# An RWKV-7 and token-mixing kernel: v of the first eight tiles loaded in long runs and turned back by TensorE, the last output row in two column parts

## The chip, the core and the metric

The kernel runs on one core of one Trainium2 chip. Its time is the device time of one execution in microseconds (us). The core has five engines that run side by side and wait for each other by semaphores: PE (TensorE, matrix multiplies and transposes, results in PSUM), DVE (VectorE), ACT (ScalarE), POOL (GpSimd) and SP, which here only issues transfers. Sixteen DMA engines carry the transfers of SP's and POOL's queues. PSUM has eight banks.

## The reference, cut to what matters

A recurrent state of 40 x 40 is kept for each of 4 batches and 8 heads over 768 steps; its read-out is the input of a token-mixing layer over 320 channels.

```python
for t in range(S):                                   # S = 768, D = 40
    y[:, :, t] = einsum('bhd,bhde->bhe', r[t], state)
    Sa = einsum('bhde,bhe->bhd', state, a[t])
    state = state * w[t] - einsum('bhd,bhe->bhde', Sa, b[t]) + einsum('bhd,bhe->bhde', v[t], k[t])
x = y as [4, 768, 320]
theta = x @ w_theta
y2 = einsum('ts,bsd->btd', w_tok_r, x * cos(theta)) + einsum('ts,bsd->btd', w_tok_i, x * sin(theta))
u = x + y2
out = u + maximum(u @ w_ch, 0)
```

The six inputs r, k, v, w, a, b are fp32, [4, 8, 768, 40] each: a head's step is a run of 40 numbers (160 bytes), and the steps of one head follow each other in memory.

## The kernel before, in words

**Tiles.** The work is cut into 24 tiles of 128 steps, six to a batch, tile i = 6 * batch + position. For a tile, w, k, b, a and v are each loaded with the 128 steps on the partitions and the eight heads side by side, 160 KB in 1024 runs of 160 bytes (`load`, L497, issued at L635). r is loaded differently, for two tiles at once (a pair): eight successive steps of a head lie together in memory, so a partition takes a run of 1280 bytes (L644, two issues of 128 runs for a pair). The rows then stand in another order, eight steps on one partition; one copy makes bf16 of them (L715), eight PE transposes turn them (L723), and two strided copies on ACT put each tile's steps in order (L727), which gives r transposed. r is needed in that form only.

**One tile's work.** `prep` (L653): ACT takes the log of w (L659), PE sums it over the steps (L666 to L674), ACT exponentiates (`ex`, L678). k, b and a are multiplied by the result on POOL (L686, L690; on DVE for the first two tiles). v is copied to bf16 as it lies (L695, on ACT for tiles 0 and 1, on POOL after). PE transposes k and b, a and v (L616) and ACT copies the results out of PSUM (L619: kbT, aT, vT). v is needed in both forms: transposed for the scores against r (`lamv`), and as it lies as a multiplier in the recurrence (x0 at L779, the state update gt at L809). `attention_scores`, `recurrence` and `readout` follow: four 128 x 1024 masked products on DVE (L745), x0, nu, the state gt, and the read-out y, which becomes x (L879). `theta` (L888) and the sines (L912, ACT) give z = x * cos and x * sin (L924, POOL). The sines need another ACT table than log and exp; a switch is a table load (L912, L1039).

**Rows.** When a batch's six tiles have their z, its six output rows of 128 steps can be made (`mix_row`, L932): 12 matmuls of 320 columns with w_tok (L942), u = x + row (L952), three transposes of u (L843) and a copy (L619, uT), three matmuls with w_ch (L888), out = max + u (L961, `oo`), and the store (L964, SP). w_tok is loaded by POOL's queue in six blocks (L982) and transposed on PE (L990) during the first six tiles. The rows of one batch are worked on while the next batch's tiles go on.

**Order.** Every step is an operation of a planner (`Plan.order`, L98). It simulates the five engines with the costs given to `add`, and at each turn takes the ready operation of an engine with the lowest priority number, where waiting costs `WAIT` and a table switch `TSWITCH`. A priority is the tile's or row's base time (`TIMES`) plus the kind's offset (`OFF`) plus a number for the single operation (`ADJ`). The result is a fixed instruction order for each engine and each queue; SP's loads are ordered in the same way, and a load also waits until its buffer is free (raw_v has six, one a tile). A PSUM bank is taken when a PE operation starts and freed when its readers are done; single banks are four. Some operations of the start have dummy matmuls put before them (`WARM`).

Of the kernel before, what the change touches and what calls it, by code (L numbers as in the profile page):

```python
# [24 lines left out]
SP_DEPTH = 3600.0  # L25
WARM = {("tv", 0): (512, 512, 512, 512, 512, 512, 256), ("cs", 0): (256, 128),
# [205 lines left out]
def tail(n):  # L232
# [4 lines left out]
    ah=-35.84, ch=48.62, cs=-41.07, ea=8.9, egd=-133.96, egt=-68.6, ekb=29.91, enu=-49.74,  # L237
    enut=-31.32, er=-1.07, eth=-44.84, eut=-81.74, ev=34.77, ewt=-21.29, ex=-16.18, exp=-69.77,
    ext=-70.75, gd=-0.66, gt=24.57, kb=0.69, la=-21.49, lb=-20.79, lk=-21.05, ln=-58.38,
    loadr=-19.57, lv=-18.31, lw=-23.25, mlu=77.8, mlv=20.57, mphi=99.76, mpsi=106.6, nu=-4.03,  # L240
    nut=17.1, nx=-102.76, oo=44.39, r=13.19, row=39.85, sin=86.4, slu=-21.92, slv=29.13,
    sphi=-34.9, spsi=-25.62, st=34.46, ta=-13.27, th=35.87, tkb=6.76, tr=-5.45, tv=13.16,
    uadd=-11.95, ut=33.59, v=-54.81, wdma=85.37, wt=32.27, x0=-18.91, xt=5.58, y=-25.18,
    z=50.36)
WAIT, TSWITCH, PSWITCH = 398.44, 188399.0, -3357.0
TIMES = dict(
    tile=[
        -65.18, -52.14, -27.19, -15.19, -0.09, 16.27, 18.34, 39.82, 40.75, 43.08, 49.45, 52.18,
        68.94, 83.98, 96.98, 120.81, 109.42, 127.8, 136.07, 145.79, 151.2, 162.31, 163.45,
        185.34],  # L250
    row=[
        43.16, 28.13, 30.47, 7.23, 53.69, 54.58, 93.52, 93.6, 115.41, 121.11, 101.85, 144.65,
        150.48, 155.04, 152.8, 117.63, 86.15, 91.69, 209.97, 231.59, 245.27, 311.99, 320.81,
        183.2],
    rel=[
        -80.1, 35.36, 62.13, 56.14, -154.77, 90.95, 23.01, 50.8])
ADJ = {
    0: 0.01, 1: -0.88, 2: -0.27, 3: -0.13, 4: -9.48, 5: 1.93, 6: 0.01, 7: -6.64, 8: -6.95,
    9: 2.16, 10: -0.5, 11: 4.59, 12: 0.14, 13: 0.14, 14: -2.05, 15: 1.86, 16: 1.1, 17: 0.1,
    18: 0.09, 19: -1.57, 20: -11.2, 21: 2.84, 22: -9.69, 23: 4.35, 24: 11.96, 25: -7.67,  # L260
    26: -8.16, 27: -0.64, 28: 7.64, 29: -2.2, 30: 9.61, 31: -5.25, 32: -7.79, 33: 1.01,
    34: 0.1, 35: 13.97, 36: 2.59, 37: 8.9, 38: -2.75, 39: -7.81, 40: -5.57, 41: -1.21,
    42: -0.06, 43: 0.97, 44: 0.99, 45: 4.55, 46: -1.08, 47: 23.46, 48: 0.44, 49: 12.19,
    50: -0.53, 51: 9.26, 52: -2.79, 53: 0.97, 54: -23.89, 55: 7.88, 56: 2.16, 57: 5.54,
    58: 1.4, 59: 0.22, 60: 1.28, 61: -5.88, 62: -2, 63: -5.35, 64: 13.13, 65: -1, 66: 0.41,
    67: -1.73, 68: 4.62, 69: -0.84, 70: -7.71, 71: -0.16, 72: 4.87, 73: -0.18, 74: 3.79,
    75: 4.43, 76: 0.74, 77: 0.06, 78: 6.38, 79: -6, 80: -2.91, 81: 0.43, 82: 3.27, 83: 3.51,
    84: -0.44, 85: -2.07, 86: -2.74, 87: -2.44, 88: 2.94, 89: -22.98, 90: 3.09, 91: 9.21,
    92: -2.91, 93: 18.56, 94: 11.17, 95: -1.31, 96: -4.33, 97: -0.08, 98: 3.45, 99: 0.12,
    100: -1.86, 101: -0.16, 102: -12.32, 103: 7.19, 104: -6.11, 105: 0.71, 106: -14.73,  # L270
    107: -16.11, 108: -1.26, 109: -2.12, 110: -11.67, 111: 2.03, 112: -15.5, 113: -2.82,
    114: -4.71, 115: -1.47, 116: -2.37, 117: -4.76, 118: 13.45, 119: 10.68, 120: -10.01,
    121: 0.33, 122: 3.27, 123: -1.43, 124: 0.58, 125: -0.44, 126: -0.16, 127: -0.19,
    128: -0.03, 129: 9.47, 130: 3.96, 131: -3.42, 132: 7.74, 133: 20.39, 134: -13.3, 135: -2.8,
# [796 lines left out]
```

## Time and profile before

| | us |
|---|---|
| median of 7 executions | 213.9 (212.45 to 214.21) |
| profiled execution, device time | 213.41 |
| its span, first to last instruction | 211.6 |
| PE busy / ACT busy / POOL busy | 198.8 / 152.6 / 117.6 |
| hardware queue (SP): share of the 16 DMA engines' time | 66.8% |

How to read it: an engine is busy while one of its instructions runs; PE's matmuls overlap, so busy does not mean at its peak. PEld is PE's loading of weights beside the matmuls. The DMA share is the mean busy share of the sixteen DMA engines in a stretch. A group line gives line, engine, operation, written and read tile, shape and count, then total busy us and mean ns of one, then idle time before them with what ended it. The chain of waits follows from the last instruction back to what released each step: start, length, what.

### The profile page before, as it was taken

Reading aid. Unit: us, or ns where it says so; the run is one execution under the profiler, and the core shown is the slowest. Engines: PE = TensorE matmul, PEld = TensorE weight load, DVE = VectorE, ACT = ScalarE, POOL = GpSimd, SP = SyncE. Lnnn points to the kernel's source line nnn. Section 1 sums busy time; section 2 is a strip of 40 time slices with the busy share of each in tenths; the row PEclk is TensorE's granted clock in tenths of the full one; section 3 lists DMA queues with packets and bytes.
Section 4 is the critical chain, followed back from the end, with each engine's and each line's share of the span. In section 5 each row is a group of like instructions: output and inputs, shape, how many; then the busy total and the mean of one; then the engine's idle time right before and its main releaser. Section 6 shows DMA issues by size and latency. Waiting matters only on the chain.

```text
span 211.6 us, 8102 instructions
## 1 busy us (share of the span) xinstructions
PE 198.8 (94%) x3365; PEld 155.4 (73%) x3365; DVE 166.3 (79%) x253; ACT 152.6 (72%) x342; POOL 117.6 (56%) x173
## 2 busy tenths in 40 slices
PE   7787999979999999999999999999999999999993
PEld 3465787757777788788787877788778787877761
DVE  7587778896979799789898677877889898946343
ACT  4475777999799868977948789777898757573011
POOL 3205365779878674885971859773658440751000
PEclk9999999999999999999999999999999999999998
DMA  7999999899999999995989889989895101002122
GB/s 121 196 159 193 158 190 180 136 199 179 181 175 181 187 188 203 187 165 68 260 160 194 166 155 211 161 183 174 187 197 111 34 3 33 2 3 94 67 91 93
DMA packets 134181, 30.82 MB, mean 146 GB/s; under 512 B 125824, under 2 KB 134144, under 8 KB 134144
## 3 DMA queue, kind: packets, MB, share of 16 engines
q1 hardware_dynamic: 131712, 27.54, 66.8%
q0 software_dynamic: 2432, 2.77, 8.6%
q8 instruction: 26, 0.43, 0.9%
q14 instruction: 11, 0.09, 0.1%
HBM read 29.13 MB, written 3.93 MB: 156 GB/s over the span
## 4 chain that ended last, share of the span: by engine, by line
PE 73%; DMA 8%; POOL 6%; SPq 6%; ACT 3%; issue 2%; DVE 0%; POOLq 0%; ACTq 0%; DVEq 0%
PE ps_s L942 19%; PE ps_s L616 12%; PE ps_d L740 9%; PE ps_s L888 9%; SPq L635 5%; PE ps_s L843 4%; POOL kb L686 3%; DMA wrow_r<-in_moe_w_tok_r_dram 3%; DMA raw_v<-in_v_dram 2%; DMA raw_w<-in_w_dram 2%; PE ps_s L723 2%; PE ps_s L809 2%; PE ps_s L791 2%; PE ps_s L990 2%; PE ps_s L872 2%
## 5 line engine op out<-in xcount | busy, mean ns | idle before, releaser
L686 POOL TENSOR_TENSOR kb<-raw_kb,ex 128x320 bf16<-128x320 f32 x44 | 37.2, 862 | 17.5 <-ACT ex L678 17.3
L942 PE MATMUL ps_s<-zr,wtok_r 128*128 128x320 bf16 x144 | 41.0, 300 | 0.0
L942 PE MATMUL ps_s<-zi,wtok_i 128*128 128x320 bf16 x144 | 40.9, 299 | 0.0
L690 POOL TENSOR_TENSOR ah<-raw_a,ex 128x320 bf16<-128x320 f32 x22 | 19.0, 864 | 29.6 <-issue 15.6
L745 DVE TENSOR_TENSOR lamu<-ps_d,mask_p 128x1024 bf16<-128x1024 f32 x24 | 29.3, 1220 | 7.5 <-PE ps_d L740 7.1
L745 DVE TENSOR_TENSOR phi<-ps_d,mask_n 128x1024 bf16<-128x1024 f32 x24 | 29.2, 1219 | 4.5 <-PE ps_d L740 4.2
L745 DVE TENSOR_TENSOR lamv<-ps_d,mask_p 128x1024 bf16<-128x1024 f32 x24 | 29.2, 1218 | 4.0 <-PE ps_d L740 3.8
L745 DVE TENSOR_TENSOR psi<-ps_d,mask_p 128x1024 bf16<-128x1024 f32 x24 | 29.2, 1216 | 1.5 <-PE ps_d L740 1.5
L924 POOL TENSOR_TENSOR zi<-cs,x 128x320 bf16<-128x320 f32 x23 | 17.7, 790 | 10.1 <-ACT cs L912 9.9
L924 POOL TENSOR_TENSOR zr<-cs,x 128x320 bf16<-128x320 f32 x23 | 17.7, 791 | 6.8 <-ACT cs L912 6.8
L678 ACT ACTIVATE ex<-ps_d 128x648 f32<-128x648 f32 x24 | 17.1, 713 | 4.8 <-PE ps_d L674 3.6
L619 ACT COPY uT<-ps_s 128x192 f32<-128x192 f32 x24 | 7.5, 318 | 15.5 <-PE ps_s L843 14.2
L879 DVE TENSOR_TENSOR x<-ps_s,ex 128x320 bf16<-128x320 f32 x24 | 11.7, 486 | 8.1 <-PE ps_s L872 4.0
L942 PEld LDWEIGHTS <-wtok_r 128*128 128x128 bf16 x144 | 14.0, 98 | 4.5
L740 PE MATMUL ps_d<-aT,kbT 64*128 64x128 bf16 x384 | 16.6, 218 | 0.8 <-ACT kbT L619 0.7
L942 PEld LDWEIGHTS <-wtok_i 128*128 128x128 bf16 x144 | 14.1, 98 | 3.5
L619 ACT COPY kbT<-ps_s 128x512 f32<-128x512 f32 x24 | 14.2, 590 | 3.3 <-PE ps_s L616 3.1
L952 DVE TENSOR_TENSOR u<-ps_s,x 128x320 bf16<-128x320 f32 x24 | 11.7, 489 | 6.0 <-PE ps_s L942 5.3
L961 DVE SCALAR_TENSOR_TENSOR oo<-ps_s,u 128x320 f32<-128x320 f32 x24 | 11.6, 488 | 5.2 <-PE ps_s L888 4.3
L616 PE MATMUL ps_s<-ident,kb 128*128 128x128 bf16 x192 | 14.7, 219 | 0.8 <-POOL kb L686 0.7
L870 PE MATMUL ps_s<-kb,lamv 128*128 128x40 bf16 x192 | 15.4, 180 | 0.0
L872 PE MATMUL ps_s<-kb,lamu 128*128 128x40 bf16 x192 | 15.0, 180 | 0.3 <-DVE lamu L745 0.2
(117 smaller groups left out, 561.9 us busy)
## 6 DMA issues: line engine op xcount, KB each, us to landing
raw_v<-in_v_dram SPq DMA_DIRECT2D x24, 160.0 KB, 3.6
raw_w<-in_w_dram SPq DMA_DIRECT2D x24, 160.0 KB, 4.4
raw_kb<-in_k_dram SPq DMA_DIRECT2D x24, 160.0 KB, 4.1
raw_a<-in_a_dram SPq DMA_DIRECT2D x24, 160.0 KB, 4.0
raw_kb<-in_b_dram SPq DMA_DIRECT2D x24, 160.0 KB, 4.3
raw_r<-in_r_dram SPq DMA_DIRECT2D x24, 160.0 KB, 3.7
out_dram<-oo SPq DMA_DIRECT2D x24, 160.0 KB, 1.9
wrow_i<-in_moe_w_tok_i_dram POOLq DMA_DIRECT2D x6, 192.0 KB, 5.2
```

Source lines behind the costliest of these rows:

```text
L616: nc.tensor.transpose(out=dst[:, c:c + 128], in_=pair(src, g), identity=ident)
L619: nc.scalar.copy(out=out.bitcast(FP32), in_=in_)
L678: add("ACT", "exp", i, lambda: nc.scalar.activation(out=ex, in_=ps(pk).rearrange("p a b -> p (a b)")[:, 512 - DM:512 + DM + 8], func=AF.Ex ...
L686: lambda j=j: (nc.vector if fast else nc.gpsimd).tensor_tensor(out=paired(kb[:, j])[:, :, :, 0:D], in0=natural(raw_kb[s4][:, j]), in1=invW ...
L690: lambda: (nc.vector if fast else nc.gpsimd).tensor_tensor(out=paired(ah)[:, :, :, 0:D], in0=natural(raw_a[i % 6]), in1=Wi, op=ALU.mult),
L740: nc.tensor.matmul(t[:, q, g, :], lhsT=lhs[rows(q), g * 128:(g + 1) * 128], rhs=rhs[rows(q), g * 128:(g + 1) * 128], start=True, stop=True)
L745: add("DVE", kindm, i, lambda: nc.vector.tensor_tensor(out=dst.rearrange("p a b c -> p (a b) c"), in0=ps(p).rearrange("p a (g c) -> p (a g ...
L870: nc.tensor.matmul(o, lhsT=lamv[:, p, g, :], rhs=kb[:, 0, h, 0:D], start=first, stop=False, skip_group_check=True)
L872: nc.tensor.matmul(o, lhsT=lamu[:, p, g, :], rhs=kb[:, 1, h, 0:D], start=False, stop=True, skip_group_check=True)
L888: nc.tensor.matmul(dst, lhsT=lhs[:, kt, :], rhs=rhs[:, kt, :], start=kt == 0, stop=kt == 2)
L924: nc.vector if fast else nc.gpsimd).tensor_tensor(
L942: nc.tensor.matmul(ps(pk)[:, 0:DM], lhsT=wtok[nm][:, s, j * 128:(j + 1) * 128], rhs=zs[c][:, s], start=n == 0 and c == 0, stop=n == NT - 1 ...
```

## The change

v of tiles 0 to 7 (`V_PAIRS = 4` pairs) is loaded as r is: for a pair, two issues of 128 runs of 1280 bytes. `turn_pair`, made out of the function that read r, casts the pair in one copy (on ACT for pair 0, on POOL for pairs 1 to 3) into one buffer `v8`, turns it with eight transposes and copies each tile's vT with the strided form on ACT. Since v is also needed as it lies, four PE transposes per tile turn vT back (`tn`) and one ACT copy (`en`) puts it into v. The tiles 8 to 23 load v as before. raw_v becomes three pair buffers of the same total size.

The last output row (batch 3, row 5) is made in two column parts, 0 to 127 and 128 to 319: each part has its own row matmuls, u, transposes and uT copy; then come the two parts of the product with w_ch, of `oo`, and of the store.

All planner numbers are new: `OFF`, `WAIT`, `TSWITCH`, `PSWITCH`, `TIMES` and the some 1,470 of `ADJ`. The costs, latencies and `WARM` are the same.

```diff
+V_PAIRS = 4
...
-WAIT, TSWITCH, PSWITCH = 398.44, 188399.0, -3357.0
+WAIT, TSWITCH, PSWITCH = 564.9, 2520797.0, -1529.0
...
-    raw_v = sb("raw_v", [128, H, D], FP32, 6)
+    raw_v = sb("raw_v", [128, 2, 8 * D], FP32, 3)
...
+    v8_t = padded("v8", [128, 8, 2, 64], 1, last24)[0]
...
+    lu_t = [consts.tile([128, 128 + 128 * h], BF16, name=f"lu_{h}") for h in range(2)]
+    nc.vector.memset(lu_t[1][:, DM - 128:], 0.0)
...
         for key, dst, src in load(i):
+            if key[0] == "raw_v" and i < 2 * V_PAIRS:
+                continue
...
+            s = i // 2
+            for kind, nm, ap, dst, base in (("loadr", "raw_r", r, raw_r[s % 2], s % 2),
+                                            ("lv", "raw_v", v, raw_v[s % 3], None)):
+                if kind == "lv" and s >= V_PAIRS:
+                    continue
+                rr = ap[bi, :, ci * C:(ci + 2) * C, :].rearrange(
+                    "(c g) (t q) d -> c t g (q d)", c=2, q=8)
+                for c in range(2):
+                    key = (nm, s % 2, c) if base is not None else (nm, (i + c) % 6)
+                    add("SP", kind, i,
+                        lambda c=c, rr=rr, dst=dst: nc.sync.dma_start(out=dst[:, c], in_=rr[c]),
+                        600, [], [key], work=520)
...
-        add("ACT" if fast else "POOL", "v", i,
+        if i >= 2 * V_PAIRS:
+            add("ACT" if fast else "POOL", "v", i,
...
-        tr("tv", "ev", (vb,), vT_t[i % NTR], [("v", i % NRV)], ("vT", i % NTR), "ACT")
+        if i >= 2 * V_PAIRS:
+            tr("tv", "ev", (vb,), vT_t[i % NTR], [("v", i % NRV)], ("vT", i % NTR), "ACT")
+        else:
+            if i % 2 == 0:
+                turn_pair(i, "v", "tv", "ev", v8_t, ("v8", 0), raw_v[i // 2 % 3],
+                          [("raw_v", i % 6), ("raw_v", (i + 1) % 6)],
+                          [(vT_t[(i + x) % NTR], ("vT", (i + x) % NTR)) for x in range(2)])
+            vT = vT_t[i % NTR]
+            pv = ("ps", "tn", i)
+
+            def back():
+                t = ps(pv).bitcast(BF16)
+                for g in range(G):
+                    nc.tensor.transpose(out=t[:, g * 128:(g + 1) * 128],
+                                        in_=vT[:, g * 128:(g + 1) * 128], identity=ident)
+            add("PE", "tn", i, back, 4 * mm(128), [("vT", i % NTR)], [pv], new=(pv, 1),
+                tail=tail(128))
+            evac("ACT", "en", i, pv, vb.rearrange("p h d -> p (h d)"), 512,
+                 writes=[("v", i % NRV)])
...
+    def last_row(bi, j):
...
+        parts = ((0, 128), (128, DM))
+        for h, (lo, hi) in enumerate(parts):
+            n = hi - lo
+            kts = (hi + 127) // 128 - lo // 128
+            pk = ("ps", "row", q, h)
+            for s in range(NT):
+                def chunk(s=s, pk=pk, lo=lo, hi=hi):
+                    for c, nm in enumerate("ri"):
+                        nc.tensor.matmul(ps(pk)[:, 0:hi - lo],
+                                         lhsT=wtok[nm][:, s, j * 128:(j + 1) * 128],
+                                         rhs=zs[c][:, s, lo:hi], start=s == 0 and c == 0,
+                                         stop=s == NT - 1 and c == 1)
...
+            add("DVE", "uadd", q, lambda pk=pk, u=u, lo=lo, hi=hi: nc.vector.tensor_tensor(
+                out=u[:, 0:hi - lo], in0=ps(pk)[:, 0:hi - lo], in1=x[:, lo:hi], op=ALU.add),
+                155 + 1.04 * n, [pk, ("x", q % NX)], [("lu", h)], at="row")
...
+            add("PE", "ut", q, turn, kts * mm(128), [("lu", h)], [p], at="row", new=(p, 1),
+                tail=tail(128))
+            add("ACT", "eut", q, lambda p=p, uT=uT, kts=kts: copy_words(
+                uT.rearrange("p a b -> p (a b)"), ps(p)[:, 0:64 * kts]),
+                165 + 53 * kts, [p], [("luT", h)], at="row")
+        for h, (lo, hi) in enumerate(parts):
...
+            add("PE", "ch", q, ch, 3 * mm(hi - lo),
+                [("luT", 0), ("luT", 1), ("wch", 0), ("wch", 1)], [ck], at="row", new=(ck, 1),
+                tail=tail(hi - lo))
...
+            add("SP", "st", q, lambda oo=oo, lo=lo, hi=hi: nc.sync.dma_start(
+                out=out_r[bi, j][:, lo:hi], in_=oo), 350, [("loo", h)], [], at="row", work=300)
...
-            mix_row(bi, j)
+            (last_row if bi == B - 1 and j == NT - 1 else mix_row)(bi, j)
```

## The prediction

> **What bounds the kernel now.** I read the page first (busy shares, slices), then busy time by stretch, the chain of waits, the timeline of single engines, the groups by form, and last the trace's packet records.
>
> ```profile
> span 211.6 us, 8102 instructions
> ...
> PE 198.8 (94%) x3365; PEld 155.4 (73%) x3365; DVE 166.3 (79%) x253; ACT 152.6 (72%) x342; POOL 117.6 (56%) x173
> ...
> DMA  7999999899999999995989889989895101002122
> ```
>
> One number for the whole run misleads: the DMA engines are full for some 150 us and empty afterwards, while PE is busy throughout. Busy time by stretch separates two regimes:
>
> ```profile
> core 0: us, PE busy (x) PEld busy (x) DVE busy (x) ACT busy (x) POOL busy (x), PEclk, DMA share, GB/s
> 20.00:60.00 40.00, 36.78 (x733) 29.95 (x732) 32.30 (x35) 33.63 (x80) 28.17 (x41) 1.00 0.97 175
> 72.00:140.00 68.00, 67.95 (x1182) 54.65 (x1181) 56.37 (x75) 54.03 (x118) 47.43 (x67) 1.00 0.96 177
> ```
>
> From 72 us on PE has work at every moment (67.95 of 68 us): the rows of finished batches fill it, so the end is set by how much PE work is left at that point. Before, PE lacks work. In 20 to 60 us it is idle for 3.2 us by its busy time; spacing of matmul starts above the median of their form shows about 9 us lost between 20 and 70 us. What it waits for there:
>
> ```profile
> 11.55 4.79 DMA raw_w<-in_w_dram
> ...
> 56.59 5.15 DMA raw_v<-in_v_dram
> 61.80 0.45 POOL v L695
> 62.25 0.37 POOL wrow_r L982
> 62.78 0.39 POOL v L695
> 63.17 6.24 DMA wrow_r<-in_moe_w_tok_r_dram
> 69.46 0.84 PE ps_s L990 x12
> 71.55 1.09 PE ps_s L942 x8
> ```
>
> The chain enters and leaves this stage through transfers: the last w_tok block lands at 69.4, its transposes follow at once, and at 71.55 the rows of the first batch begin. On ACT the third tile's w is used as it lands (16.42, after 0.76 us of waiting for it); tiles 3 to 6 take w 0.3 to 1.0 us after landing (for example landed 22.0, used 23.0). Loading is just in time up to about 57 us, when the last load of tiles 0 to 7 lands.
>
> **The change, part by part.**
>
> *v in runs of 1280 bytes, tiles 0 to 7.* In the packet records 122,880 packets of 160 bytes take 14.9 ns each, 6,144 of 1280 bytes 66.5 ns. A 160 KB load is 1024 of the first (1024 x 14.9 / 16 engines = 0.95 us of the stream) or 128 of the second (0.53 us). Eight loads: 8 x 0.42 = 3.4 us less transfer before 57 us. The number of SP issues stays (two per pair), but v of the odd tile moves ahead of that tile's w, k, a and b: an even tile needs 4 x 0.95 + 4 x 0.53 = 5.9 us of stream (now 5.8), an odd one 3.8 (now 4.8). Bounds: 0 if something else paces the stage, 3.4 if all of it arrives. I take 3.4 here and set the costs against it.
>
> ```profile
> L727 ACT COPY rT<-ps_s 128x512 bf16<-128x512 bf16 x24 | 14.1, 602 | 0.2
> ...
> L619 ACT COPY vT<-ps_s 128x256 f32<-128x256 f32 x24 | 9.3, 388 | 0.0
> ```
>
> *Copies on ACT.* The two groups above give the forms (busy us, mean ns of one). Eight vT copies take the strided form of rT: 8 x (602 - 388) = 1.7 us. Eight new copies back into v (the form of vT): 8 x 388 = 3.1 us. The cast of pair 0 replaces two: 728 - 2 x 458 = -0.2 us. Together +4.6 us, 3.6 of it for tiles 2 to 7, inside 20 to 60 us, where ACT is idle for 6.4 of 40 us. The new copy waits for PE's turn back; behind it in ACT's queue stand the exps, kbT and nx copies for which POOL and PE wait. Bounds on the path: 0 (it fits in the gaps) to 3.6 (none does). The nearest row is 40 to 50 us, where ACT reaches 9.47 of 10: at that share 33.6 + 3.6 = 37.2 us of work need 39.3, so the stage cannot shrink by more than 0.7 of its 2.6 us (3.4 less the 0.8 that is saved before tile 2). That is a charge of 1.9. Against it, two table loads of 1283 ns stand in this stage (41.09, 47.43), and the new planner constants make a switch dearer; if they leave, the charge falls towards 0. I take 1.4.
>
> *PE.* Tile transposes stay 32; 32 turn v back: 32 x 56 ns (median spacing) = 1.8 us, all before 60 us. Charge 0, covered by the 9 us lost there; 1.8 if that cover is gone.
>
> *POOL and DVE.* POOL loses six v casts (448 ns each by their group) and gains three pair casts (713, the group of r): -0.5 us, charge 0, as POOL waits for ACT's exp there. DVE zeroes two more tiles (218 + 85 ns). Its zeroing ends at 5.48 and it then waits until 6.43 for the first exp, so 0; at most 0.3.
>
> *The v that PE multiplies comes later.* After the cast come eight transposes (0.6), two copies (1.2), four transposes (0.4), a copy (0.4): some 2.6 us more before x0 and gt can start. For tile 0 v landed at 3.64 and x0 starts at 11.83, after psi's mask; ACT is idle for 2.2 us between 3.6 and 9.5 and the added copies need 1.5 before x0. Bounds 0 to 1.5; I take 0.4, near the lower end since the time from landing to use is 8 us.
>
> *Last row in two parts.* Row columns stay the same (12 x 136 ns against 12 x (56 + 83)). The end now, on DVE:
>
> ```profile
> 206.40 0.49 DVE L952 TENSOR_TENSOR u<-ps_s,x 128x320 bf16<-128x320 f32 x1 [1.32 <-PE ps_s L942]
> 206.81 0.48 DVE L961 SCALAR_TENSOR_TENSOR oo<-ps_s,u 128x320 f32<-128x320 f32 x1
> 207.94 0.90 DVE L961 SCALAR_TENSOR_TENSOR oo<-ps_s,u 128x320 f32<-128x320 f32 x2 [0.65 <-PE ps_s L888]
> ```
>
> Between u and the last oo stand three transposes, the 0.32 us copy to uT and three matmuls of 136 ns; two rows share this tail, hence two oo. Of the last row only the later part stays on it: u and oo on 192 columns (0.49 to about 0.36 us each, an estimate: a fixed 0.15 us and the rest by width), one transpose (0.06) and a fifth of the copy (0.07) less: -0.4. The second store queues behind the first on SP, 0.36 us an issue; the parts' results are 0.25 to 0.3 apart, so +0.1. Net -0.3; bounds -0.4 to +0.4.
>
> *The order.* Every offset is new, so all queues are reordered. No row prices that; I allow 1.5 us either way and take 0.
>
> Sum: -3.4 + 1.4 + 0 + 0.4 - 0.3 = -1.9 us. The profiled execution took 213.4 (span 211.6 and 1.8 around it), 0.5 below the median of 213.9; on the median this gives 212.0.
>
> **Two rules of the Trainium skill.** "Perfetto Trace Analysis", Identifying the Most-Contended Engine, judges DMA by HBM use against 358 GB/s, not by engine occupancy, and says to work on the most contended engine. By it the stage's 175 GB/s is an estimated 49% and ACT at 84% is the one to relieve, so the 3.4 us vanish, ACT's cost remains, and the sum would be +1.5 us. The landings used within 1 us speak for the occupancy of 0.97. "DMA: Bandwidth & Descriptors", Why small descriptors are slow, gives about 3 cycles per packet beside its 32-byte beats: 8 x 8 = 64 cycles against 43, a third saved; an estimate of 2.5 us where the packets show 3.4.
>
> **Rivals.**
> *ACT becomes the bound (slower).* Place: 20 to 60 us. If ACT cannot rise above its present 84%, 37.2 us of work take 44.2: +4.2 - 0.3, 217.8. At 93% the stage keeps its 40 us; below that the change loses. Half way, at 88.5%, 42.0: +2.0 - 0.3, 215.6. For it: 17.9 of 20 busy in 40 to 60. Against it: 7.9 of 10 in 20 to 40, and the table loads can move.
> *Hidden.* POOL's w_tok issue (62.25, behind a v cast of tile 8, still in short runs) gates the rows at 71.55; if it keeps its place, the relief ends as PE idle time and only the tail's -0.3 is left: 213.6. Against it: that issue itself waited behind a transfer.
> *All of it arrives.* -3.4 - 0.4: 210.1; with a table pair gone from a full ACT, or a luckier order, 209.
>
> **Numbers.** A measurement tells about 0.5% (1.1 us) from no change. Relief partly arrives: 0.44, 212.0 (210.8 to 212.8). All arrives: 0.14, 210.1. Hidden: 0.14, 213.6. ACT or the order makes it slower: 0.28, 215.6. Range 209.2 to 216.4: it leaves out the worst ACT cases and orders better than all of the relief. Faster 0.57 (the first two, less a sliver), same 0.15, slower 0.28. Both signs hold much, so the likeliest one's own range stands above.
>
> **What would show it.** Packets of 160 bytes fall by 8192; the first row matmuls begin near 69 instead of 71.55; ACT's share in 20 to 60 rises to 90% or more; rT-like v copies near 600 ns; four more PE transposes a tile; a final oo near 0.36 us. It is wrong if rows begin no earlier while ACT fills up, or if PE shows gaps after 72 us.

## The result and the profile after

The changed kernel took 215.46 us (median of 15 executions, 214.53 to 218.34); the kernel before, run beside it on the same chips, took 213.63 us (36 executions, 212.15 to 215.01). The ratio is 1.0098, with a 95% interval of 1.0073 to 1.0123: slower by about 1%, 1.8 us on the medians. The forecast was 212.0, faster. The profiled execution took 215.17 (span 213.4) against 213.41 (211.6) before.

The page of the changed kernel, the lines that answer to those shown of before:

```profile
span 213.4 us, 8206 instructions
...
PE 199.4 (93%) x3412; PEld 159.2 (75%) x3412; DVE 167.7 (79%) x257; ACT 152.8 (72%) x348; POOL 117.4 (55%) x170
...
DMA  6997999999999989949999989999961001001321
```

The totals hardly say anything: every engine is as busy as before within 1.4 us, apart from PE's weight loads (3.8 us more). Busy time by stretch, same columns as before:

```profile
core 0: us, PE busy (x) PEld busy (x) DVE busy (x) ACT busy (x) POOL busy (x), PEclk, DMA share, GB/s
20.00:60.00 40.00, 38.05 (x772) 31.49 (x769) 32.28 (x36) 33.44 (x85) 24.96 (x34) 1.00 0.97 183
72.00:140.00 68.00, 66.87 (x1189) 54.68 (x1189) 56.00 (x73) 54.71 (x120) 48.69 (x69) 1.00 0.92 171
```

Two things differ. Between 20 and 60 us PE is busier than before (38.05 against 36.78 us). From 72 us on, where it never lacked work before (idle 0.05 of 68 us), it is now idle for 1.13 us. The chain of waits (start, length, what) shows where:

```profile
79.31 0.44 POOL kb L706
...
80.08 0.59 POOL wrow_i L1077
80.67 0.52 POOL wrow_r L1077
81.19 6.63 DMA wrow_r<-in_moe_w_tok_r_dram
87.82 0.05 issue
87.87 0.84 PE ps_s L1085 x12
```

and PE's own timeline (start, busy, line, operation; in brackets the idle time before and its releaser) shows what it cost:

```profile
86.46 0.39 PE L629 MATMUL ps_s<-ident,ah 128*128 128x128 bf16 x4
87.87 0.51 PE L1085 MATMUL ps_s<-ident,wrow_r 128*128 128x128 bf16 x6 [1.02 <-DMA wrow_r<-in_moe_w_tok_r_dram]
```

PE stands for 1.02 us before the transposes of a w_tok block. POOL issues three w_tok transfers in a row from 80.08; the third lands at 87.8, 6.6 us later. The one PE needs (block 1 of the real part) had been issued at 62.2 before; the new order put it behind two others at 81.2.

To see when the time was lost I counted PE's useful work: the matmuls begun up to a moment, each at the median spacing of its form, without the 32 transposes that turn v back (1.8 us).

```
useful PE work done, us, at      20     40     60     70     85     90    200
before                         7.01  22.47  36.48  43.86  57.58  62.34 163.91
after                          6.37  20.92  36.57  44.28  57.51  60.94 162.67
after, lead                   -0.64  -1.55  +0.09  +0.42  -0.07  -1.40  -1.24
```

Part of the lag at 20 us is PE's clock. The trace's records grant the full clock from 8.17 us on, in the kernel before from 5.27; until then matmuls start 1.9 times as far apart as later. The same eight transposes before and after:

```profile
7.62 0.61 PE L616 MATMUL ps_s<-ident,kb 128*128 128x128 bf16 x8
...
7.10 1.06 PE L629 MATMUL ps_s<-ident,kb 128*128 128x128 bf16 x8
```

Up to 85 us nothing is lost: what the changed kernel is behind at 40 us it has made up by 60. Then 1.3 us go at the one wait, and they never return, because from there PE has work all the time; "PE shows gaps after 72 us" was one of the prediction's own signs of being wrong. The rest is at the end: the last row's matmul starts 1.43 us later than before (207.43 against 206.00), the span ends 1.75 us later.

The parts of the change are there as described. The two forms of copies of v (mean ns of one after the bar's busy time):

```profile
L632 ACT COPY vT<-ps_s 128x256 f32<-128x256 f32 x16 | 6.1, 382 | 0.0
L768 ACT COPY vT<-ps_s 128x512 bf16<-128x512 bf16 x8 | 4.7, 605 | 0.3 <-PE ps_s L764 0.3
L632 ACT COPY v<-ps_s 128x256 f32<-128x256 f32 x8 | 3.0, 399 | 0.0
```

Packets of 160 bytes fell by 8,192 to 114,688. But the first row's matmuls begin at 77.5 instead of 71.4, and ACT's share in 20 to 60 us is 84% (33.44 of 40), as before.

On the spread: a ratio, here and below, leaves out executions more than 1.5% above their kernel's fastest, a median does not, so that of the changed kernel's five executions at 217.0 to 218.3 us (at a lower granted TensorE clock, 0.987 to 0.991 over the span) three are in its ratio, while three like them of the fourth run below (217.2 to 217.5) are not in its own; the median of the other eleven here is 215.1, 1.5 us above before, that of the other nine there 213.3, 0.1 below. The last section takes this up.

### The profile page after: what moved, and what is told of

Its sections match the earlier page's. It is cut to its first block, busy times and chain, and to the rows that moved or that the text cites. A ratio compares the mean times of both kernels' runs of the same rounds, so it can differ in the third digit from the quotient of the medians.

```text
span 213.4 us, 8206 instructions
## 1 busy us (share of the span) xinstructions
PE 199.4 (93%) x3412; PEld 159.2 (75%) x3412; DVE 167.7 (79%) x257; ACT 152.8 (72%) x348; POOL 117.4 (55%) x170
## 4 chain that ended last, share of the span: by engine, by line
PE 66%; DMA 12%; SPq 8%; POOL 5%; issue 4%; ACT 3%; DVE 1%; POOLq 0%; ACTq 0%; DVEq 0%
PE ps_s L1037 17%; PE ps_s L629 10%; PE ps_d L781 9%; PE ps_s L929 8%; SPq L650 5%; DMA raw_r<-in_r_dram 4%; PE ps_s L884 3%; DMA wrow_r<-in_moe_w_tok_r_dram 3%; SPq L664 3%; POOL kb L706 3%; DMA raw_kb<-in_k_dram 3%; DMA raw_w<-in_w_dram 2%; PE ps_s L850 2%; PE ps_s L832 2%; PE ps_s L1085 2%
## 5 line engine op out<-in xcount | busy, mean ns | idle before, releaser
L1037 PE MATMUL ps_s<-zr,wtok_r 128*128 128x320 bf16 x138 | 39.2, 300 | 0.0
L1037 PE MATMUL ps_s<-zi,wtok_i 128*128 128x320 bf16 x138 | 39.1, 299 | 0.0
L965 POOL TENSOR_TENSOR zi<-cs,x 128x320 bf16<-128x320 f32 x23 | 18.2, 802 | 14.0 <-DVE lamv L786 13.5
L965 POOL TENSOR_TENSOR zr<-cs,x 128x320 bf16<-128x320 f32 x23 | 18.2, 803 | 8.0 <-ACT cs L953 7.9
L781 PE MATMUL ps_d<-aT,kbT 64*128 64x128 bf16 x384 | 17.3, 218 | 0.6 <-DVE lamu L786 0.3
L1037 PEld LDWEIGHTS <-wtok_r 128*128 128x128 bf16 x138 | 13.4, 97 | 4.4
L629 PE MATMUL ps_s<-ident,kb 128*128 128x128 bf16 x192 | 15.4, 224 | 1.1 <-POOL kb L706 1.0
L756 POOL CAST r<-raw_r 128x640 bf16<-128x640 f32 x11 | 7.9, 717 | 14.9 <-DMA raw_r<-in_r_dram 14.9
L1037 PEld LDWEIGHTS <-wtok_i 128*128 128x128 bf16 x138 | 13.5, 98 | 3.3
L768 ACT COPY rT<-ps_s 128x512 bf16<-128x512 bf16 x24 | 13.8, 599 | 2.1 <-PE ps_s L764 2.0
```

Of the source, the lines that this page charges most:

```text
L629: nc.tensor.transpose(out=dst[:, c:c + 128], in_=pair(src, g), identity=ident)
L768: add("ACT", ke, i + x, lambda x=x, dst=dst: nc.scalar.copy(out=dst.rearrange("p (g t q) -> p g t q", g=G, q=8), in_=ps(pr).bitcast(BF16). ...
L781: nc.tensor.matmul(t[:, q, g, :], lhsT=lhs[rows(q), g * 128:(g + 1) * 128], rhs=rhs[rows(q), g * 128:(g + 1) * 128], start=True, stop=True)
L965: nc.vector if fast else nc.gpsimd).tensor_tensor(
L1037: nc.tensor.matmul(ps(pk)[:, 0:DM], lhsT=wtok[nm][:, s, j * 128:(j + 1) * 128], rhs=zs[c][:, s], start=n == 0 and c == 0, stop=n == NT - 1 ...
```

## Experiments

Times are medians; a ratio is to the kernel before, run on the same chip.

### The long runs alone, in the old order

```diff
         # load(i), tiles 0 to 7; nothing is turned or put in order
+        if i < 8:
+            c0 = ci - ci % 2
+            vsrc = v[bi, :, c0 * C:(c0 + 2) * C, :].rearrange(
+                "(c g) (t q) d -> c t g (q d)", c=2, q=8)[ci % 2]
+            vdst = raw_v[i % 6].rearrange("p h d -> p (h d)")
```

> The kernel before, every engine's order unchanged, but v of tiles 0 to 7 loaded in 128 runs of 1280 bytes; v is not brought back into its order, so the v that is used is not the reference's. It is the transfer relief alone (3.4 us of the stream by packet times). Theory A, transfers pace the first 57 us: 210.5 to 212.0 (-1.6 to -3.1). Theory C, the relief is worth little because other engines pace the stage: 213.0 to 213.9.

Measured: 212.56 us, ratio 0.9963 (0.9945 to 0.998): the relief by itself is worth 0.8 us, a quarter of the 3.4. The transfers do land earlier: tile 5's v at 38.7 instead of 43.6, tile 9's at 59.6 instead of 62.6. What then ends last is something else. Before, the shares of the chain of waits by engine were PE 73%, DMA 8%, POOL 6%, SP's queue 6%, ACT 3%. With the long runs alone the chain could be followed back only to 37.6 us, so that the shares sum to 80%:

```profile
PE 70%; DVE 5%; ACT 3%; issue 2%; POOL 0%; ACTq 0%; DVEq 0%
```

From 37.6 us to the end no transfer is left on the chain, where before it had those of v (56.59) and w_tok (63.17); DVE's masked products, ACT's exponentials and PE's scores of the recurrence took their place:

```profile
41.11 1.21 DVE phi L751
42.81 1.23 DVE lamv L751
...
58.85 1.24 DVE phi L751
61.34 1.28 ACT L918
```

What set the pace before 37.6 us this chain does not say. In 20 to 60 us PE gained only 0.42 us on the 36.78 of before:

```profile
core 0: us, PE busy (x) PEld busy (x) DVE busy (x) ACT busy (x) POOL busy (x), PEclk, DMA share, GB/s
20.00:60.00 40.00, 37.20 (x739) 30.47 (x738) 32.82 (x36) 34.11 (x81) 28.57 (x41) 1.00 0.96 183
```

### The new order with short runs

```diff
+                    if kind == "lv":     # 1024 runs of 160 bytes into the same buffer
+                        nc.sync.dma_start(
+                            out=dst[:, c].rearrange("p (h d) -> p h d", h=H),
+                            in_=v[bi, :, (ci+c)*C:(ci+c+1)*C, :].rearrange("h t d -> t h d"))
```

> The changed kernel, every order unchanged, turn and turn-back kept, but v of tiles 0 to 7 loaded again in runs of 160 bytes (its values stand in the wrong order, so the output is not the reference's). Theory A: the relief is real and lost elsewhere, so without it 217 to 219 (+1.5 to +3.4 over 215.5). Theory C: 215.2 to 216.2.

Measured: 216.16 us, ratio 1.008 (1.0047 to 1.0113), by the ratio not to be told from the changed kernel's 1.0098 (median 215.46). Taken alone this says that the relief is worth nothing in the new order; a later run corrects that.

### The new order without turning v back

```diff
-                t = ps(pv).bitcast(BF16)
-                for g in range(G): nc.tensor.transpose(...)
+                pass
...
-            evac("ACT", "en", i, pv, vb.rearrange("p h d -> p (h d)"), 512, ...)
+            add("ACT", "en", i, lambda: None, 165 + 512 / 2.4, ...)
```

v of these tiles stays zero; POOL zeroes it at 2.8 to 4.7 us, when it has nothing else to do.

> The changed kernel, orders unchanged, without the 32 transposes and 8 copies that turn v back (v of tiles 0 to 7 stays zero, so the output is not the reference's; zeroed at the start by POOL). Theory B, the turn-back work on ACT and PE eats the gain: 212 to 213.5. Theory D, a wait that the new order put behind it (w_tok block 1 at 87.9 us, 1.3 us of PE work) sets the loss: 215.0 to 215.5, since the work before 70 us does not reach the end.

Measured: 214.3 us, 1.0036 (1.0003 to 1.007). About 0.6%, 1.3 us (the intervals allow 0.4 to 2.2), come back, near the 1.4 that the prediction charged. Whether that is a cost of its own or the same loss at 87 us seen from another side, the ninth run asks.

### The late w_tok transfer moved forward

```diff
     order = plan.order()
+    loads_w = [o for o in order if o.kind == "wdma"]
+    late = [o for o in loads_w if o.i == 3][-1]
+    order.remove(late)
+    order.insert(order.index([o for o in loads_w if o.i == 4][-1]) + 1, late)
```

> The changed kernel with one move: the transfer of w_tok_r's block 1, which POOL issues at 81.2 us as the third of three in a row, is issued right after the one at 66 us; its buffer is free by then. Theory D, PE's stand from 86.9 to 87.9 and what follows from it are lost because of that late transfer: -1.0 to -1.4, 214.1 to 214.5. Theory B or C (loss made before 70 us): 215.2 to 215.7.

Measured: 214.02 us, 1.0014 (0.9984 to 1.0043). One transfer issued 12 us earlier takes 0.84% away, 1.8 us (the intervals allow 1.0 to 2.7) of the 2.1 that the ratio 1.0098 stands for; between the medians without the longest executions it is 1.7, of a loss of 1.5. This is the main cause of the loss.

### The v change put into the old order by hand

The instruction order of the kernel before, with v's new operations inserted beside the old ones; last row whole.

```diff
 order of before, tiles 0 to 7:
-  SP  v(i)             POOL v(i)         PE tv(i)   ACT ev(i)
+  SP  v(pair) x2       POOL v(pair)      PE tv(pair)   ACT ev(pair) x2
+  PE  tn(i)   ACT en(i)     ahead of x0(i)
```

> The kernel before with every operation in its old place and bank, and only the v change put in: the second load of a pair right behind the first, the pair's cast and transposes where the even tile's stood, both strided copies behind them, the turn-back just ahead of its use; the last row whole. Theory D (the new order made the loss): the v change by itself costs little, relief 0.8 against about 1.3 of turn-back, 213.4 to 214.4. Theory B (the turn-back work is the loss): 215 to 216.5. If transfers paced the stage: below 212.5.

Measured: 219.26 us, 1.0233 (1.0186 to 1.028), where 213.4 to 214.4 was expected: a miss. Its busy times in 40 to 60 us:

```profile
core 0: us, PE busy (x) PEld busy (x) DVE busy (x) ACT busy (x) POOL busy (x), PEclk, DMA share, GB/s
40.00:60.00 20.00, 16.45 (x321) 13.28 (x318) 13.60 (x15) 18.90 (x42) 14.60 (x19) 1.00 1.00 182
```

ACT reaches 18.90 of 20 us and PE falls to 16.45. In the old order, which keeps the first sines and their two table loads (at 46.6 and 52.6 us here) in this stretch, the added copies do fill ACT. But this is only a part of the loss. By the count of useful PE work above, the profile is behind the kernel before by 2.4 us at 20 us, 3.2 at 40, 5.1 at 60 and 8.1 at 200, so 2.0 of 8.1 us fall in this stretch. The first 2.4 go while PE has half its clock: the full clock is granted from 17.42 us on here, from 5.27 before. The profiled execution was the longest of the six (221.55); whether the others started in the same way is not on record. A better hand order may exist, so this bounds nothing; it shows that put into the old order in this way the change costs more than it saves. That the full ACT is why the new order has no sines before 61.9 us is likely, but not shown.

### The parts of the split row put at the end

```diff
 end of the order:
-  ... row 22, row 21 | u 22, u 21, ch 22, ch 21, oo, st, oo, st      (row 23's parts stored near 198 us)
+  ... row 22, row 21, row 23 part 1, row 23 part 0 | u, ut, ch 1, ch 0, oo, st, oo, st
```

> The changed kernel with the two parts of the last row moved from the place that the planner gave them (12 us before the end) to the very end, behind rows 21 and 22. If two short parts shorten the tail as the prediction had it: -0.3 to -0.6 (214.6 to 214.9 where the changed kernel gives 215.2). If the tail is set by the engines' latency and not by the width of the row: 215.0 to 215.6.

Measured: 217.77 us, 1.0179 (1.0117 to 1.0241). From the last row matmul to the end it takes 5.44 us (209.75 to 215.19) instead of 5.96, so short parts do shorten that stretch; but the last row matmul comes 2.3 us later than in the changed kernel. Why it comes so much later was not traced.

### The first sines back in their old place, on top of the moved transfer

```diff
 on the kernel with the w_tok transfer moved forward, tiles 0 to 2:
-  ACT sin x4 at 61.8 to 68.5, POOL z x12 at 62 to 76
+  ACT two of the sines at 49.5 to 52.3, POOL z x4 at 50.7 to 54.4, z x2 at 62 (one more pair of table loads)
```

> The kernel with the w_tok block moved (f1), and also the sines of the first three tiles and their products z moved from about 60 to about 46 us, as they stood before the change; that brings back one pair of table loads (2.6 us of ACT) in the stage of 40 to 60 us. If the bunch of table load and four sines at 60 to 68 us starves PE (idle 0.6 of 2 us at 62): 212.3 to 213.0 against f1's 213.2 to 214.0. If ACT's fullness in 40 to 60 us is what counts: 214.5 to 215.5.

Measured: 219.95 us, 1.0287 (1.0239 to 1.0334).

```profile
core 0: us, PE busy (x) PEld busy (x) DVE busy (x) ACT busy (x) POOL busy (x), PEclk, DMA share, GB/s
40.00:60.00 20.00, 16.82 (x304) 14.42 (x299) 13.02 (x13) 18.43 (x40) 11.83 (x16) 0.83 0.98 186
```

The same picture as with the order of before: ACT at 18.43 of 20, PE down to 16.82, and the granted clock at 0.83 after a stand of 2.28 us. The half clock lasted 6.83 us (51.28 to 58.11) and has its part in PE's loss. Moved forward in this way the sines cost more than they save; that their late place is harmless is not shown by it.

### The w_tok issues ahead of tile 8's v cast, in the kernel before

```diff
 POOL's order of before, at 57 to 63 us:
-  v(8), wdma, v(9), wdma, wdma
+  wdma, wdma, wdma, v(8), v(9)
```

> The kernel before with three w_tok transfers issued by POOL ahead of tile 8's cast of v instead of behind it (the cast waits for its load until 61.8 us). If that wait delays the rows as the chain of waits shows it: rows start up to 1 us earlier, 212.6 to 213.2. If the transfers then only take the place of the loads: 213.2 to 214.0.

Measured: 213.91 us, 1.0001 (0.9971 to 1.0031); rows begin at 72.2. The rival called "hidden" rested on this gate: it is none. In the profile the three issues begin at 61.89 instead of 62.19 us, since the products kb that stand ahead of them on POOL end no earlier, and the chain of waits from there to the rows' start names POOL, ACT, PE and DVE but no transfer: something else ends as late.

### The moved transfer together with no turning back

The edits of the third and fourth runs together.

> The new order with the late w_tok transfer of block 1 moved 12 us forward (as in the run that gave 1.0014), and v of tiles 0 to 7 not turned back: 32 TensorE transposes and eight ACT copies fewer, so that the first tiles multiply zeros in place of v. Theory S (the losses add up: 1.3 us for turning back, 1.8 us for the late transfer, and the shorter stream pays what it paid in the old order): 214.0 - 1.3 = 212.7, ratio about 0.995. Rival O (both edits take away the same loss: PE simply had 1.3 to 1.8 us too little work in reach before 90 us, and either edit gives it back): ratio 1.001, 214.0, as with the transfer alone. Rival R (without both, all of the predicted relief appears): 211.5 or less, ratio 0.99.

Measured: 214.49 us, 1.0059 (1.0025 to 1.0092), against 1.0014 with the transfer alone. The two gains do not add up; leaving 32 transposes and eight copies out brings nothing once the transfer is early. So turning back has no price of 1.3 us that is its own; the third run may have seen the wait at 87 us from another side, but its profile doesn't settle that. Why this run is somewhat above the fourth is open.

### The eight copies on VectorE

```diff
-            evac("ACT", "en", i, pv, vb.rearrange("p h d -> p (h d)"), 512,
+            evac("DVE", "en", i, pv, vb.rearrange("p h d -> p (h d)"), 512,
```

with the transfer moved as in the fourth run.

> The same order as the run that gave 1.0014 (late w_tok transfer moved forward), with the eight copies that put the turned v back made on VectorE in place of ScalarE, at the same places of the order; TensorE's turns stay. Theory A (what turning back costs is ScalarE's time in 20 to 60 us, 97% full with it): the copies cost nothing on VectorE, which is busy 32 of 40 us there, and about 1 us is gained: ratio 0.996 to 0.998, 213.0 to 213.4. Rival P (the price is in the latency of the turn and in TensorE's queue, whichever engine copies): ratio 1.001, 214.0. Rival V (VectorE's masked updates set the pace of this stage, so that eight copies more there cost more than on ScalarE): ratio 1.005 or more, 215.

Measured: 213.82 us, 1.0023 (1.0 to 1.0046). The ratio gains nothing over 1.0014, though ACT is busy for 16.66 instead of 18.04 us in 40 to 60. Its longest of 12 executions took 214.7 us, where three of 12 took over 217 with the copies on ACT; but the next run, which has them on VectorE too, again took over 217 us in four of 12, so the copies are not shown to be the reason. The profile has no wait left at the old place:

```profile
85.78 0.39 PE L837 MATMUL ps_s<-ident,ah 128*128 128x128 bf16 x4
86.00 0.50 PE L1293 MATMUL ps_s<-ident,wrow_r 128*128 128x128 bf16 x6
```

By the same count as above its useful PE work at 60, 90 and 200 us is 37.05, 62.74 and 164.46: ahead of the kernel before by 0.57, 0.40 and 0.55 us. Yet its span is 211.5 against 211.6. What PE gained by 200 us is gone at the end.

### One row at the end instead of two

```diff
 end of the order:
-  row 22, row 21 mixed | u 22, ut 22, u 21, ut 21, ch 22, ch 21, oo 22, st, oo 21, st
+  row 21, u 21, row 22, ut 21, ch 21 | u 22, oo 21, st, ut 22, ch 22, oo 22, st
```

> The kernel with the eight copies on VectorE and the late w_tok transfer moved forward (1.0023), with the last two rows reordered: row 21's matmuls are finished before row 22's, so that only row 22 stands at the end and row 21's last products (ch) run while row 22's u is made. Theory T (the tail lost 0.35 us because two rows, 22 and 21, end there side by side: their two u stand one behind the other on VectorE, 0.27 us, and the two last oo take 1.12 us together where one takes 0.48): from the last row matmul to the end 5.3 us or less where it was 5.94, and 0.5 us less in all: ratio about 1.000. Rival (what sets the end is the store's landing and TensorE's remaining products, the same in either order): no change, 1.002, 5.9 us.

Measured: 215.19 us, 1.006 (1.0027 to 1.0093), and from the last row matmul to the end still 5.97 us (210.50 to 216.47). The theory falls. One row alone has the same chain as two side by side:

```profile
210.89 0.50 DVE u L1255
...
211.44 0.36 PE ps_s L1092 x3
...
211.82 0.33 ACT uT L840
...
212.19 0.60 PE ps_s L1137 x3
...
212.81 0.49 DVE oo L1264
```

From u's start to oo's end this takes 2.41 us; in the kernel before the same chain (206.40 to 208.84) took 2.44. The difference had to lie behind it. Looking at when the last store lands and when the span ends, all kernels fall into two groups:

```
                                          last store landed   span ends   between
before                                          210.72          211.64      0.92
long runs alone, old order                      209.84          210.76      0.92
v change in the old order, row 23 whole         218.84          219.75      0.91
after                                           212.04          213.39      1.35
parts of the split row at the end               213.83          215.19      1.36
copies on VectorE                               210.18          211.52      1.34
one row at the end                              215.11          216.47      1.36
```

The instruction records of SP explain the two groups. After its last issue SP waits for its transfers, one semaphore after the other, each of some 0.06 us if it is already satisfied. In the kernel before the wait on the last store's semaphore is the last of nine (it ends at 210.77, the store having landed at 210.72); after it come only the closing drains and the barrier. In the changed kernel it is the second (212.08), and seven further semaphores, long satisfied, are gone through until 212.52: 0.44 us. SP's transfers carry eight semaphores in turn (the last three stores 108, 109, 110 before, 109, 110, 101 after), 168 transfers before and 169 after: the one store that the split row adds shifts the last store from the end of their row to its beginning.

### One store less

```diff
-    loo_t = [consts.tile([128, 128 + 64 * h], FP32, name=f"loo_{h}") for h in range(2)]
+    loo = consts.tile([128, DM], FP32, name="loo")
+    loo_t = [loo[:, 0:128], loo[:, 128:DM]]
...
-            add("SP", "st", q, lambda oo=oo, lo=lo, hi=hi: nc.sync.dma_start(
-                out=out_r[bi, j][:, lo:hi], in_=oo), 350, [("loo", h)], ...)
+            add("SP", "st", q, lambda h=h: h and nc.sync.dma_start(
+                out=out_r[bi, j], in_=loo), 350, [("loo", 0), ("loo", h)], ...)
```

on the kernel with the copies on VectorE.

> The kernel with the eight copies on VectorE and the late w_tok transfer moved forward (1.0023), with the two parts of the split row written side by side into one tile and stored whole once, near 198 us, instead of in two stores: one SP transfer fewer, everything else in the same place. Theory L (after the last store has landed SP still passes eight waits of 0.06 us each, because the 25th store shifted the numbering so that the last store is the first of them waited for; with one transfer fewer it is the last of them again): from the last store's landing to the end of the span 0.92 us as in the kernel before, where every kernel with the split row shows 1.34 to 1.39; 0.44 us less in all, ratio about 1.000. Rival (the longer end belongs to the split row or the new order as such): 1.36 us again, ratio 1.002.

Measured: 213.51 us, 0.9997 (0.9973 to 1.002), and from the last landing (211.53) to the end of the span (212.46) 0.93 us. The numbering was the cause of the longer end. With three small edits, none of which touches the arithmetic, the changed kernel is level with the kernel before; it is not faster.

### The same with short runs

The edit of the second run on the kernel just above.

> The kernel that came out level with before (late w_tok transfer forward, copies on VectorE, one store less: 0.9997), with v of tiles 0 to 7 loaded in 1024 runs of 160 bytes again, at the same places of the queue; the steps are still turned as if they lay eight to a partition, so v's values of these tiles stand at other places. Theory N (in the new order the shorter stream is worth nothing: ScalarE's and VectorE's chain and the order set the pace in 20 to 60 us): ratio 1.000, 213.3. Rival Z (the late transfer hid the relief, which shows again once it is gone, with the 0.8 us that it was worth in the old order): 1.004, 214.1. Rival F (all of the predicted 3.4 us shows): 1.016.

Measured: 216.19 us, 1.0099 (1.0061 to 1.0138), against 0.9997 with long runs: 1.0%, 2.2 us (the intervals allow 1 to 3). So in the mended order the relief is worth more than the 0.8 us of the old one. Busy time by stretch around 62 us, first with long runs, then with short ones:

```profile
60.00:62.00 2.00, 1.81 (x42) 1.34 (x40) 2.00 (x3) 1.82 (x4) 1.98 (x4) 1.00 1.12 230
62.00:64.00 2.00, 1.63 (x31) 1.28 (x30) 2.00 (x4) 1.99 (x5) 1.54 (x3) 1.00 1.13 245
64.00:66.00 2.00, 2.00 (x54) 1.73 (x50) 1.97 (x4) 2.00 (x5) 2.00 (x4) 1.00 1.12 181
66.00:68.00 2.00, 1.98 (x52) 1.71 (x50) 2.00 (x3) 1.99 (x7) 1.83 (x4) 1.00 1.09 182
```

```profile
60.00:62.00 2.00, 1.83 (x43) 1.47 (x41) 2.00 (x3) 1.82 (x5) 1.73 (x3) 1.00 1.13 191
62.00:64.00 2.00, 0.61 (x14) 0.34 (x6) 2.00 (x3) 1.99 (x4) 0.33 (x1) 1.00 1.23 216
64.00:66.00 2.00, 1.42 (x35) 1.21 (x36) 0.50 (x2) 1.11 (x2) 1.98 (x4) 1.00 1.13 278
66.00:68.00 2.00, 2.00 (x34) 1.65 (x31) 1.77 (x4) 1.65 (x3) 1.78 (x3) 0.57 1.02 163
```

With short runs PE stands for 1.97 us at 62.6 and then runs at half its clock from 66.30 to 69.71. By the count of useful work the two profiles are 0.1 us apart at 60 us and 2.6 at 70. POOL's timeline names what it waits for:

```profile
63.67 0.85 POOL L922 TENSOR_TENSOR kb<-raw_kb,ex 128x320 bf16<-128x320 f32 x1 [1.94 <-DMA raw_kb<-in_k_dram]
```

It is a load after all, k of tile 9. Its landing goes with PE's stand from profile to profile:

```
                                    k of tile 9: issued   landed   PE stands near 62 us
before                                        54.6         58.2        under 0.4
after                                         55.7         61.6        0.66
w_tok transfer moved forward                  55.8         62.2        1.53
new order with short runs                     56.5         62.6        1.48
without turning back                          56.7         63.1        2.45
both (moved forward, no turning back)         55.6         61.4        0.79
copies on VectorE                             54.3         59.0        under 0.4
one row at the end (copies on VectorE)        57.9         64.0        1.91
one store less (copies on VectorE)            54.7         59.6        under 0.4
the same with short runs                      57.0         63.5        1.97
```

So in these two profiles the loss with short runs lies in the wait for this one load and in the half clock behind it. That the shorter stream is what makes the load land in time is not shown: "one row at the end" has long runs and, up to the last two rows, the same instructions as "copies on VectorE" and "one store less", and there the load landed at 64.0 where they have 59.0 and 59.6. Nor is it shown that the turning back delays it: without turning back it landed at 63.1 and 61.4. One profile of a kernel does not tell its edit from the spread of its executions; the 2.2 us themselves rest on twelve executions of each. By the count, 0.7 us of useful work went between 60 and 70 us where the stand was 1.48, 1.7 where it was 1.53 and 2.2 where it was 1.97: the last two were followed by half the clock.

## Why the prediction was wrong, step by step

*The relief, -3.4 us.* Wrong in size. Alone it was worth 0.8 us in the old order, about 2.2 in the mended new one. The step that failed is "I take 3.4 here and set the costs against it", read from loads used within 1 us of landing. Just-in-time landings show that the transfers set the pace now; they don't show how far the next limit is. In the old order the next one, by the chain from 37.6 us on DVE's masked products with the recurrence's scores, stood 0.8 us behind. The relief should have been cut by that distance; DVE's 32.30 and ACT's 33.63 us of 40 in the same stretch hinted that it was short.

*ACT's copies, +1.4 us.* The instructions are as costed (605 and 399 ns where 602 and 388 were taken). As a charge on the path it does not stand by itself: without turning back 1.3 us came back while the late transfer was in place, none when it was not, and with the copies off ACT the ratio stayed where it was. What the copies did is at most indirect. In the old order they fill ACT (18.90 of 20 us), which is a part of that run's loss; the new one has no sines in 40 to 60 us, and the first rows begin 6 us later, where the prediction had "near 69". What they cost in the new order stays open.

*PE's turn back, 0.* Held: in 20 to 60 us PE had gaps for it, and leaving it out, together with the copies, gained nothing where the order was mended. The cover was more than the 9 us that the prediction took: by the count of useful work 13 of the 50 us from 20 to 70 were lost before.

*POOL, DVE, the later v.* Nothing in the runs speaks against the small figures, but they cannot be judged: two profiles with the same instructions at the start (copies on VectorE, one store less) differ by 1.1 us of useful PE work at 20 us, with the full clock granted from 10.14 us in one and from 13.12 in the other.

*The order, 0 with 1.5 us either way.* This step decided the sign. One w_tok transfer was put 19 us later, behind two others, in a stage where PE otherwise never waits; moving it alone brought 1.8 us. It took all of the allowed 1.5 and more, and it could not be read from the profile of before. It could have been bounded from it, though: the four w_tok transfers issued at 57 to 64 us before took 4.5 to 6.8 us to land beside the loads, and after 72 us a wait of PE is lost in full.

*The last row, -0.3 us.* Wrong in sign: +0.44 us. The step "of the last row only the later part stays on it" took the split row for the one that is worked on last. In the kernel before its products run ahead of row 22's; in the new order its parts are stored near 198 us, and rows 22 and 21 end the kernel whole. The added store moved the last store's semaphore from the last place to the second among SP's closing waits. The prediction counted the second store's issue (0.36 us) and not that.

*The sum.* Two terms of the loss are shown by taking them away, 1.8 us for the late transfer and 0.44 for the end; together they make up the measured 1.8 to 2.1 (in the profiles 1.3 and 0.44 of the span's 1.75). What is left is nothing: without these two the kernel is level with before, so the relief (2.2 us in the mended order, in part by keeping the clock up) just pays for all the rest, the turning back and the postponed sines among it. How that rest divides was not separated; its terms don't add up, as the run without turning back showed.

*The rivals.* The time fell on "ACT or the order makes it slower" (215.6 forecast, 0.28): by the order, not by ACT. ACT's share did stay at the 84% that this rival named, but the sines and two table loads had left the stage, and by 60 us PE was not behind (+0.09). "Hidden" named the wrong gate.

*The rule against the change.* The Trainium skill, "Perfetto Trace Analysis", Identifying the Most-Contended Engine, would have given +1.5 us, close to what came. Its reason fits only in part: as it has it, the transfers' full occupancy (0.97) overstated them, 0.8 of 3.4 us in the old order. But they were not free either, 2.2 us in the mended order at much the same rate (182 GB/s in 20 to 60 us), and taking load off ACT, which it would put first, left the ratio where it was.

## What to carry to other kernels

When a stream of transfers is full and its loads are used as they land, the gain from shortening it is the distance to the next limit, not the time saved on the stream; shorten the transfers alone first, leaving out what the new layout needs, and see what the chain of waits names then. A change that makes a planner write a new order is priced by that order's worst wait in the stage where the bounding engine never waits, so list every transfer that is used there with its issue and landing times in both kernels. And count the transfers: one more can shift which semaphore is waited for last at the end.

## What the runs showed of the hardware that was not expected

*A short stand of PE can lower its clock afterwards.* In the profile of the fourth run (w_tok transfer moved) PE stands for 1.53 us until 63.3. The granted clock (third number from the right):

```profile
62.00:64.00 2.00, 0.71 (x12) 0.56 (x14) 1.21 (x2) 2.00 (x4) 1.59 (x3) 0.93 1.18 248
64.00:66.00 2.00, 2.00 (x35) 1.69 (x34) 1.22 (x1) 0.58 (x3) 2.00 (x3) 0.50 1.08 220
66.00:68.00 2.00, 2.00 (x42) 1.73 (x40) 1.54 (x3) 1.42 (x3) 0.49 (x2) 0.72 1.14 199
```

That execution took 217.19 us; nine of the other eleven of the same kernel took 212.6 to 215.1. Stands of 1.91, 1.97, 2.28 and 2.45 us in other profiles were followed by the same, one of 1.48 us and all up to 1.21 us (the one at 87 us among them) were not. The one of 2.0 to 2.3 us at 2 us of the span tells nothing, since the full clock had not yet been granted there. The records change the clock only at whole steps of 3.41 us: after these stands half the clock lasted one step (63.72 to 67.13 here), after the one of 2.28 two. The length of a stand is not all that counts: with the w_tok issues ahead of tile 8's v cast the clock was 0.50 from 14.26 to 17.67 us, though PE had stood for no more than 0.53 us at a time in the step before and was busy for 2.19 of 3.41 us. The Trainium skill, "TensorE: Matmul & The Clock Gate", Part 1, lets the clock halve after one idle window of about 3.4 us; here a stand of 1.53 us within 3.41 was enough. So a wait in the middle can cost twice: itself, and 3.41 us or more at half clock. The changed kernel stands for 0.66 us in its profile. Its five longer executions have the clock of the disturbed ones, but none of them was profiled.

*The end of the kernel depends on the number of transfers.* With 168 on SP's queue 0.92 us, with 169 1.36 us from the last landing to the end of the span, by which of SP's closing waits is the last store's.

*A kernel's start is not the same each time.* Two profiles with the same instructions up to the last two rows, "copies on VectorE" and "one row at the end", have k of tile 9 landed at 59.0 and 64.0 us.

Open: what sets the landing of k of tile 9; what the turning back costs in the new order; why the run without turning back and with the early transfer (1.0059) is not below the one with the early transfer alone (1.0014), and what in the hand-made end of the sixth run held the last row matmul back by 2.3 us.
